# Turning q and k into f32 PSUM in token order with a contiguous copy-out, and moving the attention steps after the first scores one slot later

## Chip, cores, metric

One core of a Trainium2 chip. The metric is device time in microseconds of one execution. The experiments ran in three batches on three chips, each with the kernel before in the same rounds (medians 384.59, 385.45 and 384.28 us), so ratios are the sound comparison between batches. A run counts as slow when it is over 1.5% above the fastest of its kernel. A profile is of one execution. Its span is about 2 us shorter than the timed run (381.9 against 383.61 before).

In the profile's lines PE is TensorE's matmuls, PEld its weight loads, ACT is ScalarE, DVE VectorE, POOL GpSimd. PEclk is the clock granted to TensorE, in tenths of full speed. PSUM is the memory that the matmuls here write; SBUF holds the other tiles.

## The reference, cut to what matters

Attention of 4 batches, 8 heads, 768 tokens and head size 64, with a band of 16 tokens to each side and one pooled key and value for every 32 tokens. Then a gated feed-forward layer over the 3072 x 512 result, with a residual gate.

```python
scores_l = scale * q @ k.T            # only |i - j| < 16 survives
scores_s = scale * q @ k_sum.T + log(32)   # k_sum: max over blocks of 32 tokens
a = softmax(concat(scores_l, scores_s)); x = a @ concat(v, v_sum)
# x: 3072 x 512
out = x + sigmoid(x @ w_res) * ((gelu(x @ w_gate) * (x @ w_val)) @ w_out)
```

## The kernel before

The work is cut into eight units u of 384 tokens, two for each batch. A unit runs twelve gate/value blocks (`fo_step`, slots "A"), then six output steps (`out_step`, slots "B"). The attention of the next unit is woven into the "B" slots. The turning (transposing) of the next batch's k and q is woven into the "A" slots, four turns in each of units 0 to 5. I call these the gate/value phase and the output phase of a unit; k units (0, 2, 4) turn k, q units (1, 3, 5) turn q and sum v.

A q or k tile is loaded with eight consecutive tokens per partition: partition p holds tokens 8p + j. A turn therefore yields, for each j, 96 columns that belong to tokens 8p + j, and the copy out of PSUM puts them in token order.

```python
PJ = 8; PP = S // PJ                       # 8 tokens per partition, 96 partitions
# ... pools in PSUM: ps_mm 4 buffers of 512 f32, ps_s 1 of 1024, ps_o 1, ps_t 1

def transpose_pair(src, dst, pad, hp, pool, tag, copy):
    tp = pool.tile([128, PJ, PP], BF16, tag=tag, name="tp")
    for j in range(PJ):
        for hh in range(2):
            nc.tensor.transpose(tp[hh * 64:hh * 64 + 64, j, :], src[:, 2 * hp + hh, j, :],
                                ident[0:PP, 0:PP])
    o = dst[:, pad:pad + S].rearrange("d (p j) -> d j p", j=PJ)
    if copy == "act":
        nc.scalar.copy(o, tp[:])
    else:
        nc.vector.tensor_copy(o, tp[:])

# s_step: scores of two heads, Exp into P on ACT, mask on DVE.  av_step: ao = P.T @ v, then xn = ao / sum on DVE.
# xt_step: xn turned on TensorE into ps_t, copied to xT by DVE.
def out_step(u, st, gvT, sub, part):
    if part == 0:
        # ... r = xT @ w_res (4 matmuls); th = tanh(r / 2) on ACT; f = first 4 matmuls with w_out
    else:
        # ... f: the other 8 matmuls
        nc.vector.scalar_tensor_tensor(th[:], th[:], 1.0, f[:], ALU.add, ALU.mult)
        nc.vector.scalar_tensor_tensor(o[:], th[:], 0.5, st["xn"][:, sub, :], ALU.mult, ALU.add)
        # ... store o

for u in range(NU):
    # ... at half == 0: load k, q, v of the next batch on the gpsimd queue
    # ... A slots 1, 4, 7, 10: k_step (half 0) or q_step (half 1) of one pair of heads, in ps_t, copy on ACT
    for hp in range(NP):
        at(("B", hp), lambda hp=hp: s_step(u + 1, hp, nst))
        at(("B", hp + 1), lambda hp=hp: av_step(u + 1, hp, nst))
    at(("B", 4), lambda: xt_step(u + 1, 0, nst, ps_t, "t"))
    at(("B", 5), lambda: xt_step(u + 1, 1, nst, ps_t, "t"))
    for fo in range(FO):
        fo_step(st, gvT, fo)                # g, vv on TensorE; Gelu on ACT; product on DVE
        for fn in slots.get(("A", fo), []):
            fn()
    for i in range(2 * NSUB):
        for fn in slots.get(("B", i), []):
            fn()
        out_step(u, st, gvT, i // 2, i % 2)
```

In the profile's lines s are the scores, P their exponentials, ao the product of P and v, xn the attention output divided by its sums and xp that output turned in PSUM (xT is its copy). g and vv are the gate and value products, ge the Gelu of g and gvT their product; r and f are the products with w_res and w_out.

The softmax here doesn't subtract the row's maximum and nothing guards it: scores larger than these inputs give would overflow.

## Time and profile before

Before: 383.67 us median of 3 runs (382.7 to 385.25). I read the phases from the timeline of TensorE: a unit starts with its first g, its output phase with its first s.

| stretch, us from the start | length | what holds it |
|---|---|---|
| start, 0 to 54.1 | 54.1 | loads (DMA engines over 80% busy), and the chain of copies of turned q and k |
| gate/value phase of k unit 2 | 23.7 | ACT: four copies of 3.58 us ahead of the Gelus |
| gate/value phase of q units 1, 3, 5 | 24.7 | the same, and the sum of v |
| output phase of units 0 to 5 | 18.4 to 21.0 | TensorE waits 3.0 us for the first P |
| units 6 and 7 (no turns) | 31.4 and 30.8 | TensorE |

The first lines are from the page of the kernel before: busy time with share and instruction count, then two rows of the table of 40 slices, where a digit is tenths.

```profile
span 381.9 us, 6251 instructions
PE 295.3 (77%) x2640; PEld 155.7 (41%) x2640; DVE 166.1 (44%) x324; ACT 212.1 (56%) x202; POOL 70.9 (19%) x88
...
PEclk9999969987999899999999899998999989999999
DMA  8999999900100991000100994000100001000002
```

ACT is busy for only 56% of the span, and TensorE for 77%: no engine is full on average. The cause is found in the turns. These are groups by line and form: busy us, mean ns, idle before.

```profile
L261 ACT ACTIVATE ge<-g 128x384 f32<-128x384 f32 x96 | 53.0, 573 | 60.9 <-PE g L254 46.3 <-DVE gvT L262 14.6
L214 ACT ACTIVATE P<-s,bias_t 128x768 bf16<-128x768 f32 x32 | 28.8, 900 | 45.0 <-PE s L210 44.9
L171 ACT COPY kT_0_93<-tp 128x768 bf16<-128x768 bf16 x2 | 7.2, 3577 | 1.3 <-PE tp L167 1.3
L173 DVE COPY qT_3_100<-tp 128x768 bf16<-128x768 bf16 x1 | 3.6, 3557 | 0.0
```

A copy of 768 elements takes 3.58 us on ACT and 3.56 on DVE. An Exp over as many elements, written contiguously, takes 0.90. Two different engines pay the same, which points to what they have in common: the copy writes 2 bytes of every 16.

The next lines show the first turn of unit 2 in the timeline (start, length, engine, line; in brackets the idle time before it and what ended it).

```profile
147.21 0.53 PE L167 MATMUL tp<-ident,k_sb 96*64 96x96 bf16 x16
147.68 0.82 PE L254 MATMUL g<-xT,w_gate 128*128 128x384 bf16 x4
147.78 3.58 ACT L171 COPY kT_0_89<-tp 128x768 bf16<-128x768 bf16 x1 [0.63 <-PE tp L167]
150.86 1.20 ACT L261 ACTIVATE ge<-g 128x384 f32<-128x384 f32 x2
151.73 0.32 PE L254 MATMUL g<-xT,w_gate 128*128 128x384 bf16 x1 [1.28 <-ACT ge L261]
```

TensorE runs two more blocks ahead, then has no free PSUM buffer until a Gelu has read one; the Gelu stands behind the copy. The last turn of a unit does more harm, as the ACT and TensorE lines at its end show:

```profile
166.95 3.58 ACT L171 COPY kT_3_92<-tp 128x768 bf16<-128x768 bf16 x1 [1.11 <-PE tp L167]
170.03 0.83 ACT L261 ACTIVATE ge<-g 128x384 f32<-128x384 f32 x1
170.87 1.28 ACT L214 ACT_TABLE_LOAD   x1
172.17 0.90 ACT L214 ACTIVATE P<-s,bias_t 128x768 bf16<-128x768 f32 x1
...
169.67 1.03 PE L275 MATMUL f<-w_out,gvT 128*128 128x512 bf16 x4
173.71 0.38 PE L228 MATMUL ao<-vext_114,P 128*64 128x65 bf16 x12 [3.01 <-DVE P L217]
```

TensorE stands still for 3.01 us. In unit 3 the eight f matmuls take 2.92 us; after the same wait in unit 2 they took 1.90:

```profile
174.57 1.90 PE L281 MATMUL f<-w_out,gvT 128*128 128x512 bf16 x8
...
216.82 0.54 PE L228 MATMUL ao<-vext_113,P 128*64 128x65 bf16 x12 [3.01 <-DVE P L217]
...
218.16 2.92 PE L281 MATMUL f<-w_out,gvT 128*128 128x512 bf16 x8
```

In the waits view of TensorE (total us, times, longest) these two waits come first:

```profile
PE ao L228 <- DVE P L217: 18.4, 7, 3.0
PE g L254 <- ACT ge L261: 18.0, 14, 1.3
```

The Trainium skill, "TensorE: Matmul & The Clock Gate", Part 1, says that the array's clock is gated to half after an idle window of about 3.4 us that runs free of the kernel. This case agrees in kind: after the same 3.01 us wait unit 2 stayed at full clock and unit 3 did not (granted clock 1.00 from 172.5 to 176.5 us, 0.57 from 216.5 to 220.5). But the waits here are shorter than that window. The changes of the granted clock in this trace lie on a grid of 3.41 us. In the units that lost the clock, 2.0 to 3.0 us of the wait fell between two marks of the grid, and half clock began at the second; in unit 2 a mark at 172.48 cut the wait (170.70 to 173.71) into 1.78 and 1.24.

### The profile page before, as it was taken

What the parts mean: (1) busy time and instruction counts of PE and PEld (TensorE: products, weight loads), DVE (VectorE), ACT (ScalarE), POOL (GpSimd) and SP (SyncE); (2) the same over time, 40 slices, a digit from 0 to 9 for tenths busy, and PEclk for the clock granted to TensorE, in tenths of its full rate; (3) what the DMA queues carried; (4) which work ended last, traced back from release to release, by engine and by line L of the source; (5) the groups of instructions that cost most, each with busy time, mean ns of one, the idle gap of its engine ahead of it and who ended that gap; (6) DMA issues with size and microseconds to landing.
All of it is one profiled execution on the core that took longest, in us unless ns stands there. A gap on an engine that the chain in (4) does not pass through costs nothing.

```text
span 381.9 us, 6251 instructions
## 1 busy us (share of the span) xinstructions
PE 295.3 (77%) x2640; PEld 155.7 (41%) x2640; DVE 166.1 (44%) x324; ACT 212.1 (56%) x202; POOL 70.9 (19%) x88
## 2 busy tenths in 40 slices
PE   0421668669978698878978698777988699999995
PEld 0320244334544244434544344433554345645652
DVE  4044863434522264335523263435622256456432
ACT  0699317773476745785485736685376833353420
POOL 8523364000008530000007530000004100000000
PEclk9999969987999899999999899998999989999999
DMA  8999999900100991000100994000100001000002
GB/s 156 205 193 197 200 152 121 23 0 30 57 0 6 189 130 47 2 1 29 57 0 2 177 130 64 0 3 8 50 27 2 0 29 57 0 21 36 29 1 82
DMA packets 54843, 23.95 MB, mean 63 GB/s; under 512 B 37408, under 2 KB 51744, under 8 KB 54816
## 3 DMA queue, kind: packets, MB, share of 16 engines
q0 software_dynamic: 42208, 14.98, 51.6%
q1 hardware_dynamic: 8032, 7.44, 6.9%
q10 hardware_dynamic: 4576, 1.15, 1.4%
q8 instruction: 20, 0.33, 0.4%
q14 instruction: 7, 0.06, 0.0%
HBM read 32.24 MB, written 6.29 MB: 101 GB/s over the span
## 4 chain that ended last, share of the span: by engine, by line
PE 49%; ACT 24%; issue 13%; DVE 10%; ACTq 2%; DMA 1%; DVEq 0%
PE f L281 13%; PE vv L258 10%; PE g L254 8%; PE vs L188 3%; PE tp L167 3%; ACT ge L261 3%; PE r L269 2%; PE ao L228 2%; ACT L214 2%; ACTq L105 2%; PE f L275 2%; DVE P L217 2%; ACT kT_1_94 L171 2%; ACT kT_0_93 L171 2%; ACT qT_1_102 L171 2%
## 5 line engine op out<-in xcount | busy, mean ns | idle before, releaser
L254 PE MATMUL g<-xT,w_gate 128*128 128x384 bf16 x384 | 79.0, 328 | 19.3 <-ACT ge L261 18.0
L261 ACT ACTIVATE ge<-g 128x384 f32<-128x384 f32 x96 | 53.0, 573 | 60.9 <-PE g L254 46.3
L262 DVE TENSOR_TENSOR gvT<-ge,vv 128x384 bf16<-128x384 f32 x96 | 51.4, 551 | 78.3 <-ACT ge L261 45.3
L258 PE MATMUL vv<-xT,w_val 128*128 128x384 bf16 x384 | 78.6, 328 | 2.9 <-DVE gvT L262 2.9
L254 PEld LDWEIGHTS <-w_gate 128*128 128x128 bf16 x384 | 35.4, 98 | 47.2 <-issue 24.7
L214 ACT ACTIVATE P<-s,bias_t 128x768 bf16<-128x768 f32 x32 | 28.8, 900 | 45.0 <-PE s L210 44.9
L281 PE MATMUL f<-w_out,gvT 128*128 128x512 bf16 x192 | 52.4, 422 | 0.0
L258 PEld LDWEIGHTS <-w_val 128*128 128x128 bf16 x384 | 37.7, 98 | 29.7 <-issue 5.6
L195 POOL COPY vext_114<-vsum_116 32x2048 bf16<-32x2048 bf16 x6 | 11.1, 1894 | 117.0 <-DVE vsum_116 L190 117.0
L217 DVE TENSOR_TENSOR P<-P,maskt 128x768 bf16<-128x768 bf16 x32 | 20.1, 632 | 20.6 <-ACT P L214 20.5
L281 PEld LDWEIGHTS <-gvT 128*128 128x128 bf16 x192 | 18.8, 106 | 24.8 <-issue 10.3
L283 DVE SCALAR_TENSOR_TENSOR th<-th,f 128x512 f32<-128x512 f32 x24 | 16.5, 688 | 27.2 <-PE f L281 27.2
L272 ACT ACTIVATE th<-r 128x512 f32<-128x512 f32 x24 | 14.3, 594 | 25.0 <-PE r L269 24.6
L228 PEld LDWEIGHTS <-P 128*64 128x64 bf16 x384 | 9.5, 118 | 39.0 <-DVE P L217 28.9
L269 PE MATMUL r<-w_res,xT 128*128 128x512 bf16 x96 | 24.8, 381 | 0.0
L275 PE MATMUL f<-w_out,gvT 128*128 128x512 bf16 x96 | 24.6, 379 | 0.0
L195 POOL COPY vext_113<-vsum_115 32x2048 bf16<-32x2048 bf16 (+1 forms) x4 | 9.1, 2303 | 74.4 <-DVE vsum_115 L190 74.4
L292 POOL DMA_DIRECT2D vext_114<-in_v_dram x24 | 18.2, 761 | 12.9 <-DMA k_sb<-in_k_dram 5.9
L167 PE MATMUL tp<-ident,k_sb 96*64 96x96 bf16 x256 | 9.8, 227 | 12.2 <-DMA k_sb<-in_k_dram 9.6
L228 PE MATMUL ao<-vext_113,P 128*64 128x65 bf16 x192 | 6.9, 214 | 15.0 <-DVE P L217 9.0
L234 DVE TENSOR_TENSOR xn<-ao,rz 128x384 bf16<-128x384 f32 x32 | 17.8, 558 | 1.1
L167 PE MATMUL tp<-ident,q_sb 96*64 96x96 bf16 x256 | 9.8, 227 | 10.0 <-DMA q_sb<-in_q_dram 4.9
(139 smaller groups left out, 338.4 us busy)
## 6 DMA issues: line engine op xcount, KB each, us to landing
out_dram<-o SPq DMA_DIRECT2D x24, 256.0 KB, 2.0
k_sb<-in_k_dram POOLq DMA_DIRECT2D x3, 768.0 KB, 7.5
q_sb<-in_q_dram POOLq DMA_DIRECT2D x3, 768.0 KB, 10.7
vext_114<-in_v_dram POOLq DMA_DIRECT2D x20, 96.0 KB, 10.5
w_gate<-in_moe_w_gate_dram POOLq DMA_DIRECT2D x6, 256.0 KB, 14.8
w_val<-in_moe_w_val_dram POOLq DMA_DIRECT2D x6, 256.0 KB, 14.5
w_out<-in_moe_w_out_dram POOLq DMA_DIRECT2D x3, 512.0 KB, 14.0
vst<-in_v_dram ACTq DMA_DIRECT2D x5, 192.0 KB, 11.1
```

Of the source, the lines that this page charges most:

```text
L167: nc.tensor.transpose(tp[hh * 64:hh * 64 + 64, j, :], src[:, 2 * hp + hh, j, :], ident[0:PP, 0:PP])
L171: nc.scalar.copy(o, tp[:])
L214: nc.scalar.activation(P.rearrange("p a t q -> p a (t q)"), s[:, :, 0:TU], AF.Exp, scale=scale, bias=bias_t[:])
L217: nc.vector.tensor_mul(Pf, Pf, maskt.unsqueeze(1).to_broadcast([128, 2 * HT, QT]))
L228: nc.tensor.matmul(ao[64 * e:64 * e + 64, sub, hh, :], P[:, hh, t, :], vext[b % 2][:, half * HT + t, 2 * hp + hh, :], start=True, stop=Tru ...
L254: nc.tensor.matmul(g[:, 0:TU], w_gate[:, ko, fs], st["xT"][:, ko, :], start=(ko == 0), stop=(ko == KO - 1))
L258: nc.tensor.matmul(vv[:, 0:TU], w_val[:, ko, fs], st["xT"][:, ko, :], start=(ko == 0), stop=(ko == KO - 1))
L261: nc.scalar.activation(ge[:], g[:, 0:TU], AF.Gelu)
L262: nc.vector.tensor_mul(gvT[:, fo, :], ge[:], vv[:, 0:TU])
L269: nc.tensor.matmul(r[:], st["xT"][:, ko, ss], w_res[:, ko, :], start=(ko == 0), stop=(ko == KO - 1))
L275: nc.tensor.matmul(f[:], gvT[:, fo, ss], w_out[:, fo, :], start=(fo == 0), stop=False)
L281: nc.tensor.matmul(f[:], gvT[:, fo, ss], w_out[:, fo, :], start=False, stop=(fo == FO - 1))
```

## The change

Intent: write the turned columns into PSUM at their place in token order, so that the copy is contiguous on both sides. The transposes become matmuls with the identity into an f32 tile. The 768 columns of a turn are then twice as many bytes, more than the 512 f32 that are the widest tile of this pool otherwise (vs), so a turn is cut into two halves of 384 columns. And the scores after the first, all products with v and the turns of xn are moved one slot later, to give the first Exp the time of one more output step.

```diff
         def transpose_pair(src, dst, pad, hp, pool, tag, copy):
-            tp = pool.tile([128, PJ, PP], BF16, tag=tag, name="tp")
-            for j in range(PJ):
-                for hh in range(2):
-                    nc.tensor.transpose(tp[hh * 64:hh * 64 + 64, j, :], src[:, 2 * hp + hh, j, :],
-                                        ident[0:PP, 0:PP])
-            o = dst[:, pad:pad + S].rearrange("d (p j) -> d j p", j=PJ)
-            if copy == "act":
-                nc.scalar.copy(o, tp[:])
-            else:
-                nc.vector.tensor_copy(o, tp[:])
+            ph = PP // 2
+            for half in range(2):
+                tp = pool.tile([128, ph, PJ], F32, tag=tag, name="tp")
+                for j in range(PJ):
+                    for hh in range(2):
+                        nc.tensor.matmul(tp[hh * 64:hh * 64 + 64, :, j], src[:, 2 * hp + hh, j, :],
+                                         ident[0:PP, half * ph:(half + 1) * ph], start=True, stop=True,
+                                         skip_group_check=True)
+                o = dst[:, pad + half * TU:pad + (half + 1) * TU].rearrange("d (p j) -> d p j", j=PJ)
+                if copy == "act":
+                    nc.scalar.copy(o, tp[:])
+                else:
+                    nc.vector.tensor_copy(o, tp[:])
...
-                    at(("B", hp), lambda hp=hp: s_step(u + 1, hp, nst))
-                    at(("B", hp + 1), lambda hp=hp: av_step(u + 1, hp, nst))
-                at(("B", 4), lambda: xt_step(u + 1, 0, nst, ps_t, "t"))
-                at(("B", 5), lambda: xt_step(u + 1, 1, nst, ps_t, "t"))
+                    at(("B", hp + (hp > 0)), lambda hp=hp: s_step(u + 1, hp, nst))
+                    at(("B", hp + 2), lambda hp=hp: av_step(u + 1, hp, nst))
+                at(("B", 5), lambda: xt_step(u + 1, 0, nst, ps_t, "t"))
+                at(("B", 6), lambda: xt_step(u + 1, 1, nst, ps_t, "t"))
...
+            for fn in slots.get(("B", 2 * NSUB), []):
+                fn()
```

## The prediction

> **What bounds it now.** Three stretches (timeline, chain of waits).
> 1. Start, 0 to 54.1 us. The slices show DMA at 0.9 to about 50 us. From 13.9 to 39.3 us the chain is the strided copies of turned q and k on ACT (last on DVE), 3.58 us each (groups by form).
> 2. Gate/value phase of units 0 to 5. Each of four turns puts a 3.58 us ACT copy ahead of the Gelus; TensorE runs out of PSUM buffers. A three-block period is 6.39 us in k units, 5.9 in q units, for about 4.5 us of matmuls. The fourth copy delays the last Gelu, the table load (1.28) and the first Exp, so TensorE waits 3.0 us for the first P, often followed by matmuls at low clock (f: 2.9 to 3.5 instead of 1.8 us).
> 3. Units 6 and 7: no turns; TensorE-bound (34.0 and 28.05 us, windows view).
>
> **Change, costed.**
> - Removed: 32 copies of 3.58 us. The Trainium skill's "SBUF — State Buffer" (The DMA port swizzle) says SBUF has 16-byte lines and accesses crossing to a new line pay; the old copies write 2 bytes every 16. The trace agrees: 4.7 ns per element, against 900 ns for a contiguous 768-element Exp.
> - Added: 64 contiguous copies of 384 f32, estimated 0.49 us each from the Gelu of that shape.
> - 512 more weight-load/matmul pairs. 16 pairs take 0.47 us, issue-bound, so 0.47 per half turn.
> - New wait: the one-buffer pool makes the second half's matmuls wait for the first half's copy, about 0.65 us of TensorE per turn.
> - New order: P waits two output steps, not one; but the last transposes follow the last output step, whose two DVE operations (0.7 each) precede the xT copy (0.56). A hand schedule gives about 1.4 us TensorE wait at each unit start. Output phase (first scores to next g): 18.4 us before in unit 2, 16.4 after. In unit 6, without a late copy, it is 15.9 before, so the reordering alone loses about 0.5 there.
>
> **Critical path, estimated.**
> - Start: the turns finish about 15 us earlier, but only part counts: k of batch 1 queues behind the weights on the saturated DMA and lands near 53.5 us, so the first in-loop turn moves from 57.9 only to about 53.5, at a low clock after the wait. Gain about 3.
> - Gate/value phase: 23.7 to 22.4 us in k units, about 25.9 to 25.2 in q units: 6 in all.
> - Output phase: 2 us per unit plus 1.2 to 1.6 of low clock where it occurred: 16 over six units.
> - Unit 6: loses 0.5.
> Sum: about 25 us. Predicted time 358 us, range 348 to 370. Chances: faster 0.89, same 0.06, slower 0.05.
>
> **What would show it.** Copies at 0.45 to 0.6 us, ACT busy from 212 to about 130 us; the 3.0 us P wait and low-clock f stretches gone; new waits of tp on kT/qT copies (about 0.65, 24 in the loop) and of g on xT (about 1.4 per unit); in the start, tp waiting several us for k.
>
> **What would make it wrong.**
> - Each turn matmul now writes one f32 in 32 bytes. The skill's "PSUM — Partial Sum Buffer" (Specifications) says lines are 8 bytes and a non-contiguous pattern slows matmuls significantly. No trace here shows it. Twice as slow would hide under the 29 ns pair spacing, I think; several times slower would cost 1 to 2 us per turn.
> - The start could gain 10 us if k lands earlier, or none if v lands late.
> - The unit-boundary wait could be longer, or cool the clock.

## The result, and the profile after

After: 361.26 us median of 3 runs (359.93 to 361.48); before 383.67. The ratio is 0.9401, with a 95% interval of 0.934 to 0.9463. A ratio here is the mean time of one kernel's fast runs over the mean of the other's fast runs of the same rounds, so it is not quite the ratio of the medians.

The page of the kernel after, the same lines:

```profile
span 359.7 us, 7314 instructions
PE 301.2 (84%) x3152; PEld 167.7 (47%) x3152; DVE 163.7 (45%) x326; ACT 140.5 (39%) x232; POOL 71.1 (20%) x88
...
PEclk9995586999999999999999999999999999999998
DMA  8999999901000993001001995001000000001002
```

ACT lost 72 us of work, the span only 22. The clock row is new: low from about 27 to 63 us (a slice is 9 us), with a rise in between, and at 0.9 or more from there to the last slice; the dips of before, one after most of the 3.0 us waits, are gone.

The copies, from the view of the tile tp (min/median/max ns):

```profile
L174 ACT CAST kT_0_93<-tp x4: 479/479/480, 54.9 to 220.2; 128x384 bf16<-128x384 f32 x4
L176 DVE CAST qT_3_100<-tp x2: 548/549/550, 25.9 to 26.3; 128x384 bf16<-128x384 f32 x2
```

Two of 0.479 us stand for one of 3.58. The first turn of unit 2 in the timeline after:

```profile
137.70 0.53 PE L169 MATMUL tp<-ident,k_sb 96*64 96x48 bf16 x16
...
138.28 0.48 ACT L174 CAST kT_0_89<-tp 128x384 bf16<-128x384 f32 x1 [0.62 <-PE tp L169]
138.81 0.53 PE L169 MATMUL tp<-ident,k_sb 96*64 96x48 bf16 x16 [0.57 <-ACT kT_0_89 L174]
```

The second half's matmuls want the one buffer that the first half's copy is still reading: 0.57 us of idle TensorE, in every turn of the loop. The end of a unit, after:

```profile
133.40 0.69 DVE L286 SCALAR_TENSOR_TENSOR th<-th,f 128x512 f32<-128x512 f32 x1 [0.91 <-PE f L284]
133.47 0.49 PE L257 MATMUL g<-xT,w_gate 128*128 128x384 bf16 x2
134.13 0.69 DVE L288 SCALAR_TENSOR_TENSOR o<-th,xn 128x512 f32<-128x512 f32 x1
134.74 0.55 DVE L246 COPY xT<-xp 128x768 bf16<-128x768 bf16 x1
135.34 0.48 PE L257 MATMUL g<-xT,w_gate 128*128 128x384 bf16 x2 [1.38 <-DVE xT L246]
```

DVE ran these in the order of the program. The last output step's two operations stand ahead of the copy that the next unit's third matmul needs. And the start, after:

```profile
48.52 0.81 PE L261 MATMUL vv<-xT,w_val 128*128 128x384 bf16 x4
54.04 0.85 PE L169 MATMUL tp<-ident,k_sb 96*64 96x48 bf16 x16 [4.71 <-DMA k_sb<-in_k_dram]
...
56.24 1.46 PE L257 MATMUL g<-xT,w_gate 128*128 128x384 bf16 x4
```

Unit 0 starts 8 us earlier than before (46.06 against 54.10), then stands for 4.7 us until k of batch 1 has landed, and goes on at the low clock (1.46 us for four matmuls instead of 0.81).

In the waits view of TensorE the two lines shown of before are gone, and these stand in their place:

```profile
PE tp L169 <- DMA k_sb<-in_k_dram: 14.9, 2, 10.2
PE g L257 <- DVE xT L246: 9.7, 7, 1.4
...
PE tp L169 <- ACT kT_0_93 L174: 1.1, 2, 0.6
```

The first of them holds the very first load too (10.2 us), which was there before (9.6). The last is one of sixteen such lines, one for each buffer of kT and qT; together they hold the 24 waits of 0.57 us in the loop.

Where the 22.2 us of span came from, by differences of the marks (first g and first s of a unit). The 1.54 us between the early first g of the new order and where it would stand without the wait are booked to the output phase before it; that figure is the first gate/value phase of unit 6, 17.24 us with the wait, less the 15.70 it takes in the kernel before.

| term | before | after | gain |
|---|---|---|---|
| start to the output phase of unit 0 | 78.95 | 76.57 | 2.4 |
| gate/value phase, units 2 and 4 (k) | 23.73 each | 22.37 each | 2.7 |
| gate/value phase, units 1, 3, 5 (q) | 24.73 each | 25.22 each | -1.5 |
| output phase, units 0 to 5 | 119.1 in all | 16.6 each | 19.4 |
| output phase of unit 6 | 15.7 | 16.6 | -0.9 |

The first term is the least sure. The programs of the changed kernel, e1, e7 and e10 are the same up to the first g, which came at 46.06, 44.87, 44.60 and 45.84 us: the start alone varies by 1.5 us from run to run.

So nearly all of the gain is in the output phases. Of their 19.4 us, 8.8 is low clock, an estimate: before, the six took 119.1 us, and six like that of unit 2, which kept its clock, would take 110.3. The gate/value phases of units 1 to 5, where the copies sit, gave 1.2 us in all: two losses in each turn, the wait of the second half (0.57 us) and the second set of matmuls (0.46), ate what the short copies freed.

### The profile page after: what moved, and what is told of

The parts are those of the page before. It is cut to its first block, busy times and chain, and to the rows that moved or that the text cites. A ratio compares the mean times of both kernels' runs of the same rounds, so it can differ in the third digit from the quotient of the medians.

```text
span 359.7 us, 7314 instructions
## 1 busy us (share of the span) xinstructions
PE 301.2 (84%) x3152; PEld 167.7 (47%) x3152; DVE 163.7 (45%) x326; ACT 140.5 (39%) x232; POOL 71.1 (20%) x88
## 4 chain that ended last, share of the span: by engine, by line
PE 72%; DVE 9%; DMA 9%; ACT 4%; SPq 2%; issue 2%; POOL 1%; DVEq 0%; ACTq 0%
PE g L257 18%; PE vv L261 17%; PE f L284 12%; PE tp L169 7%; DMA vst<-in_v_dram 5%; PE r L272 4%; PE f L278 4%; DMA k_sb<-in_k_dram 4%; PE vs L191 4%; DVE th L286 3%; DVE o L288 3%; SPq L105 2%; PE ao L231 2%; PE s L208 2%; PE s L213 2%
## 5 line engine op out<-in xcount | busy, mean ns | idle before, releaser
L265 DVE TENSOR_TENSOR gvT<-ge,vv 128x384 bf16<-128x384 f32 x96 | 53.2, 554 | 89.6 <-PE vv L261 89.5
L257 PE MATMUL g<-xT,w_gate 128*128 128x384 bf16 x384 | 81.3, 332 | 9.7 <-DVE xT L246 9.7
L264 ACT ACTIVATE ge<-g 128x384 f32<-128x384 f32 x96 | 47.2, 491 | 103.7 <-PE g L257 60.1
L284 PE MATMUL f<-w_out,gvT 128*128 128x512 bf16 x192 | 45.4, 379 | 0.0
L169 PE MATMUL tp<-ident,k_sb 96*64 96x48 bf16 x512 | 18.4, 234 | 23.5 <-DMA k_sb<-in_k_dram 14.9
L284 PEld LDWEIGHTS <-gvT 128*128 128x128 bf16 x192 | 17.9, 98 | 20.6 <-issue 1.2
L169 PEld LDWEIGHTS <-k_sb 96*64 96x64 bf16 x512 | 14.8, 132 | 26.8 <-DMA k_sb<-in_k_dram 15.3
L169 PE MATMUL tp<-ident,q_sb 96*64 96x48 bf16 x512 | 17.5, 230 | 11.3 <-DMA q_sb<-in_q_dram 4.2
L278 PE MATMUL f<-w_out,gvT 128*128 128x512 bf16 x96 | 24.6, 379 | 0.0
L169 PEld LDWEIGHTS <-q_sb 96*64 96x64 bf16 x512 | 14.3, 128 | 18.5 <-issue 14.1
```

Source lines behind the costliest of these rows:

```text
L169: nc.tensor.matmul(tp[hh * 64:hh * 64 + 64, :, j], src[:, 2 * hp + hh, j, :], ident[0:PP, half * ph:(half + 1) * ph], start=True, stop=Tru ...
L257: nc.tensor.matmul(g[:, 0:TU], w_gate[:, ko, fs], st["xT"][:, ko, :], start=(ko == 0), stop=(ko == KO - 1))
L264: nc.scalar.activation(ge[:], g[:, 0:TU], AF.Gelu)
L265: nc.vector.tensor_mul(gvT[:, fo, :], ge[:], vv[:, 0:TU])
L278: nc.tensor.matmul(f[:], gvT[:, fo, ss], w_out[:, fo, :], start=(fo == 0), stop=False)
L284: nc.tensor.matmul(f[:], gvT[:, fo, ss], w_out[:, fo, :], start=False, stop=(fo == FO - 1))
```

## The experiments

Theory: the strided write into SBUF is the whole cost of the old copy; the change removes it and pays for that with 16 more pairs of weight load and matmul per turn, a wait for the single buffer, and a wait at each unit's start made by the slot move, which is needed only while Exp is late. Rivals stand in each expectation. Each run is the changed kernel with the edit shown, unless said otherwise. Ratios are to the kernel before, of the same rounds.

| run | median us | ratio | 95% interval |
|---|---|---|---|
| changed kernel | 361.26 | 0.9401 | 0.934 to 0.9463 |
| e1 copies only | 354.76 | 0.9234 | 0.9201 to 0.9267 |
| e2 order only | 373.24 | 0.9718 | 0.968 to 0.9755 |
| e3 read strided | 333.67 | 0.8697 | 0.8659 to 0.8734 |
| e4 PSUM contiguous | 355.65 | 0.9259 | 0.9226 to 0.9292 |
| e5 e3 with old order | 328.54 | 0.8536 | 0.8506 to 0.8566 |
| e6 k loaded early (2 of 6 runs slow) | 353.72 | 0.9153 | 0.9096 to 0.921 |
| e7 halves in two slots | 345.99 | 0.8995 | 0.8958 to 0.9031 |
| e8 halves by j | 360.3 | 0.9357 | 0.9318 to 0.9396 |
| e9 e5 with k early | 320.54 | 0.8342 | 0.8309 to 0.8375 |
| e10 xT copy first | 354.52 | 0.922 | 0.9185 to 0.9255 |

All ten gave the right result. The medians are of all runs, the ratios of the fast ones.

### e1: the new copies, the old slot order

```diff
-                    at(("B", hp + (hp > 0)), lambda hp=hp: s_step(u + 1, hp, nst))
-                    at(("B", hp + 2), lambda hp=hp: av_step(u + 1, hp, nst))
-                at(("B", 5), ...); at(("B", 6), ...)
+                    at(("B", hp), lambda hp=hp: s_step(u + 1, hp, nst))
+                    at(("B", hp + 1), lambda hp=hp: av_step(u + 1, hp, nst))
+                at(("B", 4), ...); at(("B", 5), ...)
```

> The new turns and contiguous copies with the old slot order. My theory: the copies bring the whole gain and the slot move costs about 0.5 us per unit once the first Exp is no longer late, so this is faster than the changed kernel: 357.5 us (355 to 359.5), output phase 15.9 us against 16.4, the 1.38 us wait of g on xT gone, a wait of the first ao on P of about 0.35 us per unit back. Rival: the slot move carries part of the gain by hiding the first Exp; then this is slower than the changed kernel, 363 to 370 us.

Measured 354.76 us: the copies alone are faster than the whole change, and a little below the expected range of 355 to 359.5. An output phase takes 15.72 us, and the next unit starts at once:

```profile
129.79 1.89 PE L284 MATMUL f<-w_out,gvT 128*128 128x512 bf16 x8
131.51 0.81 PE L257 MATMUL g<-xT,w_gate 128*128 128x384 bf16 x4
```

The eight f matmuls after the last transposes hide the xT copy. The slot move costs 0.9 us per unit (16.6 against 15.7), 6 us in seven units.

### e2: the old copies, the new slot order

The `transpose_pair` of the kernel before, nothing else.

> The old strided copies with the new slot order. My theory: the late Exp (3.0 us wait of the first ao) is partly covered by the extra output step of 1.7 us, leaving about 1.3 us, and the low-clock f stretches mostly go, against 1.4 us of g waiting on xT: 375 us (370 to 380), so a gain that does not add to that of the copies. Rival: the slot move costs the same 0.5 us per unit whatever the copies do: 386 to 388 us.

Measured 373.24 us, 0.9718 of before: a gain. The wait of the first ao falls from 3.01 to what the theory gave:

```profile
165.27 1.89 PE L281 MATMUL f<-w_out,gvT 128*128 128x512 bf16 x8
168.44 0.38 PE L228 MATMUL ao<-vext,P 128*64 128x65 bf16 x12 [1.28 <-DVE P L217]
```

So the same move gains 11 us with slow copies and loses 6 with fast ones. The two parts of the change work on the same wait, the late Exp, and their gains do not add: 2.8% and 7.7% alone, 6.0% together.

### e3: old transposes, strided read, contiguous write

```diff
-            o = dst[:, pad:pad + S].rearrange("d (p j) -> d j p", j=PJ)
-                nc.scalar.copy(o, tp[:])
+            o = dst[:, pad:pad + S].rearrange("d (p j) -> d p j", j=PJ)
+                nc.scalar.copy(o, tp.rearrange("d j p -> d p j"))
```

(against the `transpose_pair` of the kernel before; DVE's copy likewise, the slot order new)

> The old bf16 transposes (16 per turn, one PSUM tile), but the one copy of 768 elements reads PSUM with the stride and writes SBUF contiguously; new slot order. My theory: what costs in the old copy is the strided write into SBUF, a strided PSUM read is free or nearly so: copy about 0.8 to 1.0 us on ACT, no second half to wait for, so each of the 24 turns in the loop loses 0.46 us of matmuls and 0.57 us of wait: 336 us (332 to 345). Rival: a stride on either side costs the same: copy stays near 3.6 us and the time is that of the old copies with the new order, 370 to 380 us.

Measured 333.67 us. The tile view of tp:

```profile
L172 ACT COPY kT<-tp x16: 799/799/804, 13.8 to 213.0; 128x768 bf16<-128x768 bf16 x16
L174 DVE COPY qT<-tp x2: 947/948/948, 18.8 to 21.9; 128x768 bf16<-128x768 bf16 x2
```

The same data, the same bf16 PSUM tile, the same number of elements: 0.80 us instead of 3.58 when the stride is on the PSUM side. That settles where the old cost lay, and shows that neither f32 PSUM nor token order in PSUM was needed to remove it. The Trainium skill, "ScalarE: Activation LUTs", What ACT_TABLE_LOAD costs, gives 0.833 ns per element for an ACTIVATE, fp32 and bf16 alike; the copies agree: (799 - 479) ns over 384 elements is 0.833, with one copy reading PSUM strided and the other not. The gain over the changed kernel is 1.1 us per turn (4.41 in the four turns of unit 2), close to what was expected: 0.46 of matmuls and 0.57 of wait.

### e4: contiguous matmul writes into PSUM

```diff
-                tp = pool.tile([128, ph, PJ], F32, tag=tag, name="tp")
+                tp = pool.tile([128, PJ, ph], F32, tag=tag, name="tp")
-                        nc.tensor.matmul(tp[hh * 64:hh * 64 + 64, :, j], ...
+                        nc.tensor.matmul(tp[hh * 64:hh * 64 + 64, j, :], ...
-                    nc.scalar.copy(o, tp[:])
+                    nc.scalar.copy(o, tp.rearrange("d j p -> d p j"))
```

> As the changed kernel, but each turn matmul writes its 48 f32 contiguously into PSUM and the copy reads PSUM with the stride. My theory: the stride of the matmul write is hidden under the spacing of the pairs, so 16 pairs take 0.46 us either way, the copy stays at 0.48 to 0.6 us and the time at 361 us (358 to 366). Rival one, from the page on PSUM: the strided write slows the matmuls, so here 16 pairs take well under 0.46 us and the time falls by over 4 us. Rival two: ACT pays for the strided PSUM read, copies of 1 us and more, and the time rises above 370 us.

Measured 355.65 us: my theory falls, the first rival holds. The copy stays at 0.479 us, but the matmuls get shorter:

```profile
135.98 0.43 PE L169 MATMUL tp<-ident,k_sb 96*64 96x48 bf16 x16 [0.57 <-ACT kT L174]
136.34 0.82 PE L257 MATMUL g<-xT,w_gate 128*128 128x384 bf16 x4
```

Sixteen pairs take 0.36 us (135.98 to 136.34) against 0.46 in the changed kernel (138.81 to 139.27). So the strided write did cost: about 0.1 us in each half turn. The 48 half turns of the loop make 4.6 us (0.77 per unit) of the 5.7 by which the span is shorter; the rest lies in the start. That 16 pairs took 0.46 us both in the kernel before (96 contiguous bf16 columns each) and after (48 strided f32) was a coincidence that I had read as a limit of issuing.

### e5: e3 with the old slot order

The edits of e1 and e3 together.

> The run with the strided PSUM read, with the old slot order put back. My theory: the slot move costs 0.9 us in each of seven units whenever the copies are short (unit 1 took 41.83 us with it, 40.94 without), so 333.7 less 6.2: 327.5 us (325.5 to 329.5). Rival: the loss of the slot move came from the two-part turn at the unit start and is gone with a one-part turn: 332 to 335 us.

Measured 328.54 us, in the range of the theory: the slot move costs what it cost in e1 whatever the form of the turn.

### e6: k and q of batch 1 loaded ahead of w_res and w_out

```diff
+        k_sb[1] = load_qk(k, 1, 1, "k_sb")
+        q_sb[1] = load_qk(q, 1, 1, "q_sb")
         nc.gpsimd.dma_start(out=w_res[:], in_=moe_w_res.rearrange("(ko ki) f -> ki ko f", ki=128))
         ...
-                k_sb[nb] = load_qk(k, nb, 1, "k_sb")
-                q_sb[nb] = load_qk(q, nb, 1, "q_sb")
+                if nb > 1:
+                    k_sb[nb] = load_qk(k, nb, 1, "k_sb")
+                    q_sb[nb] = load_qk(q, nb, 1, "q_sb")
```

> The changed kernel with the loads of k and q of batch 1 issued ahead of w_res and w_out. My theory: in the changed kernel the first turn in the loop waits for k (4.7 us of idle TensorE, then about 2 us of low clock); with the load early it starts near 48.7 us instead of 54.0 and at full clock: 354.5 us (352 to 357.5), so the start gave 3.9 us where it could have given 10. Rival: something else (v, the weights, descriptor issue) holds the start and takes over at once: 359 to 363 us.

Measured 353.72 us, as the theory says. Two of the six runs count as slow (355.21 and 354.93 against the fastest, 349.48); without them the median is 353.49. The first turn of the loop no longer waits and stays at full clock:

```profile
48.71 0.53 PE L171 MATMUL tp<-ident,k_sb 96*64 96x48 bf16 x16
```

The gate/value phase of unit 0 takes 23.6 us instead of 30.5. This is the part of the start's gain that the load order held back in the changed kernel.

### e7: the two halves of a turn in two slots

```diff
-                        at(("A", 3 * hp + 1), lambda hp=hp: k_step(nb, hp, ps_t, "t"))
# ... cut: halves= passed to transpose_pair; step is k_step or q_step
+                    for i in range(2):      # one half per slot; the reduce of k after the second
+                        at(("A", 3 * hp + 1 + i), lambda hp=hp, i=i, step=step: step(nb, hp, ps_t, "t", halves=(i,)))
```

> The changed kernel with the two halves of a turn in two consecutive slots, so that a gate/value block lies between the first half's copy and the second half's matmuls. My theory: the 0.57 us wait per turn goes (24 turns, 13.7 us), about 0.1 us of gap per extra switch comes (2.4 us): 350 us (347 to 352.5). Rival: the wait only moves elsewhere (to the Gelus, since TensorE is held by ACT): 357 to 363 us.

Measured 345.99 us, better than the theory's range. The wait is real and goes; the second half of the first turn of unit 2 has none before it:

```profile
133.10 0.53 PE L169 MATMUL tp<-ident,k_sb 96*64 96x48 bf16 x16
```

Unit 1 takes 39.58 us instead of 41.83, 0.56 per turn, so the gaps that I had set against it do not appear. That is 13.5 us in 24 turns, of the 15.4 by which the span is shorter. Of the rest, 1.5 us lies before the first g, where the two programs are the same, so it is how the run's start fell; 0.5 lies in unit 0 beyond its four turns.

### e8: halves by j, a step of 16 bytes in PSUM, runs of 8 bytes in SBUF

```diff
-                tp = pool.tile([128, ph, PJ], F32, tag=tag, name="tp")
-                for j in range(PJ):
+                tp = pool.tile([128, PP, jh], F32, tag=tag, name="tp")     # jh = PJ // 2
+                for j in range(jh):
-                        nc.tensor.matmul(tp[.., :, j], src[:, 2 * hp + hh, j, :], ident[0:PP, half * ph:(half + 1) * ph], ...
+                        nc.tensor.matmul(tp[.., :, j], src[:, 2 * hp + hh, half * jh + j, :], ident[0:PP, 0:PP], ...
+                oh = o[:, :, half * jh:(half + 1) * jh]                    # four bf16 of every eight
```

> The halves of a turn are made by j instead of by p: 8 matmuls of 96 columns per half, each f32 written with a step of 16 bytes into PSUM, and the copy writes runs of four bf16 (8 bytes of every 16) into SBUF. Theory of lines: a strided PSUM write costs about 1.2 ns per element and half of the array, so 8 matmuls take 0.46 us, as 16 of 48 do; and the copy touches 96 lines with four hits each, so it stays at 0.5 to 0.6 us: 361 us (356 to 365). Rival for the matmuls: they are issue-bound, 8 take 0.23 us, 345 to 352 us. Rival for the copy: any write that is not contiguous costs 4.7 ns per element, 1.8 us: above 372 us.

Measured 360.3 us. Both halves of the theory hold:

```profile
136.19 0.48 ACT L174 CAST kT<-tp 128x384 bf16<-128x384 f32 x1 [0.62 <-PE tp L170]
136.72 0.52 PE L170 MATMUL tp<-ident,k_sb 96*64 96x96 bf16 x8 [0.57 <-ACT kT L174]
```

Eight matmuls of 96 strided columns take as long (136.72 to 137.18, where the next g starts) as sixteen of 48: the time goes with the strided elements, 384 for each half of the partitions in 0.46 us, 1.2 ns each, not with the number of instructions. (The step was 16 bytes here and 32 there, and the cost of an element the same.) And a copy whose writes leave gaps, but put four bf16 into each 16 bytes, costs 0.478 us, the same as a contiguous one. So it is not the gap that made the old copy slow, but one element per 16 bytes. Two per 16 bytes were not tried.

### e10: the last two DVE operations after the xT copy

```diff
                 # ... last 8 f matmuls of the last out_step
+                for fn in mid or []:        # xt_step(u + 1, 1): transposes and xT copy
+                    fn()
                 nc.vector.scalar_tensor_tensor(th[:], th[:], 1.0, f[:], ALU.add, ALU.mult)
```

> The changed kernel with one thing moved: the two DVE operations of the last output step come after the last xT copy instead of before it. My theory: the 1.38 us wait of g on xT at each unit start is those two operations standing ahead of the copy; with the copy first the wait is the copy itself and its latency less the two matmul groups that need no second half, about 0.6 us: 356 us (354 to 359). Rival: the wait is that of the transposes and the copy whatever stands before them: 360 to 363 us.

Measured 354.52 us. The wait at the unit's start falls from 1.38 to 0.32 us:

```profile
133.19 0.56 DVE L246 COPY xT<-xp 128x768 bf16<-128x768 bf16 x1 [1.18 <-PE xp L244]
133.80 0.48 PE L257 MATMUL g<-xT,w_gate 128*128 128x384 bf16 x2 [0.32 <-DVE xT L246]
```

A unit takes 40.77 us instead of 41.83, no longer than in e1 (40.94). So the loss of the slot move is the place of two DVE operations ahead of the copy.

### e9: what helped, together

The edits of e5 and e6.

> Strided PSUM read with one contiguous copy, the old slot order, and k and q of batch 1 loaded ahead of w_res and w_out: the three that helped, together. My theory: they add, since each takes away a different wait: 328.5 less 7.5 for the start: 321 us (318.5 to 325); TensorE should idle for nothing over 1 us after its first gate block. Rival: with the start cleared the weights or the v loads take over as the wait of the first unit: 326 to 329 us.

Measured 320.54 us, 0.8342 of before and well below the changed kernel. After the first gate block TensorE has no wait over 1 us; the longest two sums of its waits view in the loop are:

```profile
PE ao L231 <- DVE P L220: 2.5, 7, 0.4
PE xp L244 <- DVE xT L246: 1.3, 7, 0.2
```

## Why the prediction was right, point by point

- Size: 358 predicted, 361.26 measured, inside 348 to 370; faster, as given 0.89. That the sum came so close is in part luck: two of its terms were wrong by about 3.5 us each, in opposite directions (see the two phases below).
- "Copies at 0.45 to 0.6 us": 0.479 on ACT, 0.549 on DVE. Right.
- "ACT busy from 212 to about 130 us": 140.5. I subtracted whole copies, but an old copy overlapped the next instruction by half a microsecond (copy from 166.95 for 3.58, Gelu from 170.03), and busy time counts that once. That is 15 us in 30 copies; against it the Gelus, which no longer stand behind such copies, lost 8 us themselves. (Two of the 32 copies were DVE's.)
- "The 3.0 us P wait and low-clock f stretches gone": both gone; the mean of the second group of f matmuls is 379 ns against 422 before.
- "New waits of tp on kT/qT copies (about 0.65, 24 in the loop)": 0.57, in all 24; e7 shows what they cost. "g on xT (about 1.4 per unit)": 1.38, seven times; e10 shows their cause.
- "The first in-loop turn moves from 57.9 only to about 53.5 ... Gain about 3": 54.04, gain 2.4. e6 shows that the load order was the reason.
- "Output phase ... 16 over six units": 19.4. The size per unit is right (18.38 to 16.6 in unit 2), the low-clock part was larger, 8.8 us for about 4: I read it in some of the units, and five of six had it.
- "Gate/value phase: 23.7 to 22.4 us in k units, about 25.9 to 25.2 in q units: 6 in all": here the step failed. The k units went to 22.37 as said. But q units took 24.73 before, not 25.9, so they lost 0.5 instead of gaining 0.7. For units 1 to 5, as in the table above, the forecast comes to 4.7 us, and 1.2 came. The 3.4 us more in the output phases hid that miss; what is left of it is the start with unit 0 (2.4 for 3 and 1.3) and unit 6. The trace had the number; I had worked it out from one period instead of reading the mark.
- "The reordering alone loses about 0.5" per unit: 0.9. The direction was right and e1 confirms it.
- "16 pairs ... issue-bound" and "twice as slow would hide": the 0.47 us per half turn was the right number for a wrong reason. The strided PSUM write is what sets it; contiguous writes take 0.36 (e4).
- "Units 6 and 7 ... 34.0 and 28.05": I had set the boundary between them about 2.7 us late; they are 31.4 and 30.8. Nothing in the sum used them.

Not settled: how much of the start's 2.4 us is how one run's start fell. Each kernel has one profile, and the first g alone varies by 1.5 us in equal programs.

## What to carry to other kernels

When an engine's copy is slow for its element count, find which side carries the stride before rebuilding the producer: putting the stride on the PSUM read took 2.8 us off each copy by changing its access patterns alone, where moving it into the matmuls' writes cost twice the matmuls, a second buffer wait and slower writes. When a wait has been removed at its source, take out the schedule that was hiding it, and test each part alone: here one half of the change was worth 11 us without the other and cost 6 with it. And before moving work earlier in the start, check which load it will meet.

## What the Trainium skill lacked or had wrong

- "SBUF — State Buffer", The DMA port swizzle: the page says that accesses crossing to a new 16-byte line pay, without a size, and asks for at least two hits per line. The runs agree and give one: 768 bf16 writes, one per 16 bytes, took 3.58 us on ACT and 3.56 on DVE, 4.7 ns per element; four per 16 bytes (e8) cost nothing more than contiguous ones (0.478 us for 384, against 0.479).
- "PSUM — Partial Sum Buffer", Specifications: "any non-contiguous AP slows matmuls significantly" has no size. Here f32 writes with a step of 32 or of 16 bytes ran at 1.2 ns per element and half of the partitions, with two 64-column groups in turn: 0.46 us for 16 matmuls of 48 columns against 0.36 contiguous (e4), and 0.46 for 8 of 96 (e8).
- No page that I read says that a strided PSUM read is free for ACT. In e3 768 bf16 read with a step of 192 bytes took 0.799 us, and in e4 384 f32 with a step of 192 bytes the same 0.479 us as contiguous ones (on DVE 0.548 against 0.549).
- "ScalarE: Activation LUTs", What ACT_TABLE_LOAD costs: 186 ns + 0.833 ns per element for immediate scale and bias gives, as an estimate, 506 and 826 ns for 384 and 768 elements. It is stated for an ACTIVATE; the copies are recorded as CAST and COPY and took 479 and 799, so the slope agrees and their fixed part was 159 ns. The Gelu of 384 elements, an ACTIVATE, took 491 in the kernel after.
